# First query block prepared in two halves, c fetched first, one tile normalized by GpSimd: a change at the start of an attention kernel

## The chip, the core and the metric

The kernel runs on one core of a Trainium2 chip. The metric is the time of one execution in device microseconds. TensorE's granted clock, the share of full speed that the profile shows it to have been given, is listed for every run. Each ratio is between runs of the same rounds on the same chip; the profiled runs that are set side by side come from several jobs on different chips. A transfer has "landed" when all of it is there. PE is TensorE's matmuls, PEld its weight loads, DVE is VectorE, ACT is ScalarE, POOL is GpSimd, SP is the sync engine; "SPq" and "ACTq" are the queues from which those engines issue transfers.

## The reference

A block with adaptive layer norm: `c` (512 values) gives six vectors; attention over the last 512 keys of a cache (32 query heads, 8 key heads), then an MLP. Only the first steps matter here:

```python
mod = (silu(c) @ w_mod).reshape(1, 6, 1, -1)            # sa, ca, ga, sb, cb, gb
h = layernorm(x) * (1 + ca) + sa                         # x: 2048 x 512
x = x + ga * attention(h, k_cache, v_cache, wq, wo)      # q = h @ wq, 32 heads of 128
...                                                      # second layer norm, MLP with relu
```

## The kernel before

Queries are worked on in four blocks of 512. For each of 4 x 32 units (block, head) a step does score matmuls and exp, the projection of a later unit, and the products with v. Before the first step can start, the first block has to be normalized, transposed, modulated and projected. A helper records every operation and puts a wait on whatever wrote its inputs; each engine works in order (VectorE came to the three silu operations only at 7.62, behind the statistics, though the exponential they read had ended at 4.91). `warm(n)` puts n matmuls without use on TensorE, so that it is not idle.

```python
for i in range(2):                                       # x tiles 0,1 on SP; tiles 2,3 on ACT
    dma(x_sb[:, 2*i:2*i+2, :], ..., eng=ACT if i else SP)
dma(c_row, ...)                                          # SP
load_wm01(0)                                             # w_mod, contraction rows 0-255: SP
load_wm01(1, ACT)                                        # rows 256-511: ACT
load_wq(0, 2, ACT); load_wq(2, 2); load_k(0); load_v(0)  # the rest on SP
...
warm(7); silu_exp(5); warm(9)        # c transposed on TensorE, exp on ScalarE
...                                  # ScalarE: mean and variance of tile t3 (the fourth tile)
ln_stat(0); ln_stat(1); ...; ln_stat(2); ...             # VectorE
silu_mul(5)                          # VectorE: +1, reciprocal, product -> sc_bf
for tl in range(3): ln_norm(tl)      # VectorE; tile t3 is normalized by ScalarE
fs = mod_cols_mm(0, QBK)             # 32 one-column matmuls: sc_bf with both halves of w_mod
...                                  # they stand around the transposes of tile 0
for tl in range(1, TPB):
    ln_tposes(tl, [0, 2]); warm(tl)
ln_mod_ps([0, 2], hT[0], R_hT[0], 1) # four modulations, 128x512: two on VectorE, two on ScalarE
q_mms(0); q_mms(1, 5)                # projections of units 0 and 1, copies to qT by ScalarE
```

The "modulation columns" below are the 32 one-column matmuls of `mod_cols_mm`. Every one of the first outputs needs all 512 rows, so both halves of w_mod.

## Time and profile before

| | before |
|---|---|
| time, median of the first three runs | 564.28 us |
| span of the profiled run | 562.5 us |
| TensorE busy | 98% of the span |
| modulation columns start | 8.25 us |
| first score matmuls start | 13.47 us |
| span behind the first scores | 549.0 us |

The prediction shows the lines this rests on. A line of the chain reads: start, length, what the end was waiting for then. A line of the timeline reads: start, length, engine, source line, operation, output<-inputs, shape, count, and in brackets how long the engine idled and what ended that.

### The profile page before, as it was taken

Reading aid. Unit: us, or ns where it says so; the run is one execution under the profiler, and the core shown is the slowest. Engines: PE = TensorE matmul, PEld = TensorE weight load, DVE = VectorE, ACT = ScalarE, POOL = GpSimd, SP = SyncE. Lnnn points to the kernel's source line nnn. Section 1 sums busy time; section 2 is a strip of 40 time slices with the busy share of each in tenths; the row PEclk is TensorE's granted clock in tenths of the full one; section 3 lists DMA queues with packets and bytes.
Section 4 is the critical chain, followed back from the end, with each engine's and each line's share of the span. In section 5 each row is a group of like instructions: output and inputs, shape, how many; then the busy total and the mean of one; then the engine's idle time right before and its main releaser. Section 6 shows DMA issues by size and latency. Waiting matters only on the chain.

```text
span 562.5 us, 9700 instructions
## 1 busy us (share of the span) xinstructions
PE 553.7 (98%) x4097; PEld 316.9 (56%) x4172; DVE 242.2 (43%) x533; ACT 350.4 (62%) x453; POOL 38.7 (7%) x42
## 2 busy tenths in 40 slices
PE   8999999999999999999999999999999999999998
PEld 3565555555555555555555555555555654444444
DVE  4444465533334655333346553333354448321134
ACT  5986666666666666666666666666666644432500
POOL 1000000003300000033000000330000000000000
PEclk9999999999999999999999999999999999999999
DMA  9778776421331247332523522121123220210001
GB/s 268 204 165 167 143 160 132 113 38 38 39 76 37 39 93 133 57 94 46 144 56 57 102 50 39 39 40 40 39 39 72 44 31 0 41 36 24 22 28 48
DMA packets 113310, 42.70 MB, mean 76 GB/s; under 512 B 93928, under 2 KB 112104, under 8 KB 113256
## 3 DMA queue, kind: packets, MB, share of 16 engines
q1 hardware_dynamic: 112024, 40.82, 35.2%
q10 hardware_dynamic: 1232, 1.15, 0.6%
q8 instruction: 35, 0.57, 0.5%
q14 instruction: 19, 0.16, 0.1%
HBM read 18.35 MB, written 2.10 MB: 36 GB/s over the span
## 4 chain that ended last, share of the span: by engine, by line
PE 97%; issue 1%; DMA 1%; DVE 1%
PE psS L1363 28%; PE psO L1363 26%; PE psQ L1363 23%; PE psW L1363 20%; DMA x<-in_A_x_dram 1%; DVE st L1373 0%; PE psS L1366 0%; DVE mv L1374 0%; DVE rstd L1574 0%; DVE PT L1673 0%; DVE PT L1675 0%; DVE tmp L1427 0%; DVE sc_bf L1428 0%; DVE tmp L1426 0%
## 5 line engine op out<-in xcount | busy, mean ns | idle before, releaser
L1482 ACT ACTIVATE PT<-psS 128x1024 bf16<-128x1024 f32 x256 | 262.6, 1028 | 129.5 <-PE psS L1363 129.4
L1363 PE MATMUL psS<-qT,kT 128*128 128x512 bf16 x509 | 151.1, 379 | 0.2
L1363 PEld LDWEIGHTS psO<-v,PT 128*128 128x128 bf16 x2048 | 126.6, 98 | 30.2
L1363 PE MATMUL psO<-v,PT 128*128 128x129 bf16 x2048 | 137.0, 220 | 0.0
L1363 PE MATMUL psQ<-hT,wq 128*128 128x512 bf16 x507 | 130.3, 379 | 0.1
L1492 DVE RECIPROCAL rinv<-psO 128x4 f32<-128x4 f32 x128 | 23.4, 183 | 233.1 <-PE psO L1363 233.1
L1363 PE MATMUL psW<-wo,oT 128*128 128x512 bf16 x451 | 117.9, 379 | 3.2
L1493 DVE TENSOR_TENSOR o<-psO,rinv 128x512 bf16<-128x512 f32 x128 | 88.5, 692 | 4.4
L1363 PEld LDWEIGHTS psQ<-hT,wq 128*128 128x128 bf16 x508 | 49.6, 98 | 60.7 <-issue 0.5
L1363 PEld LDWEIGHTS psS<-qT,kT 128*128 128x128 bf16 x512 | 49.6, 98 | 59.3 <-ACT PT L1482 0.7
L1474 ACT ACTIVATE qT<-psQ 128x512 bf16<-128x512 f32 x127 | 75.2, 592 | 0.5 <-PE psQ L1363 0.5
L1662 ACT ACTIVATE wq<-psS 128x512 bf16<-128x512 f32 x56 | 33.4, 597 | 49.6 <-PE psS L1363 49.6
L1363 PEld LDWEIGHTS psW<-wo,oT 128*128 128x128 bf16 x512 | 45.0, 98 | 32.9 <-DVE acc L1515 1.2
L1515 DVE TENSOR_TENSOR acc<-psW,acc 128x512 f32<-128x512 f32 x48 | 33.2, 691 | 6.7 <-PE psW L1363 6.7
L1363 PE MATMUL psO<-wmw,wq 128*128 128x512 bf16 (+1 forms) x164 | 32.7, 352 | 0.3
L1518 POOL TENSOR_TENSOR acc<-acc,gaf 128x512 f32<-128x512 f32 x12 | 15.3, 1272 | 168.7 <-DVE acc L1515 168.7
L1379 POOL TENSOR_TENSOR rstd<-rstd,cst 128x4 f32<-128x4 f32 x7 | 7.1, 1012 | 265.3 <-DVE rstd L1378 265.3
L1363 PE MATMUL psS<-h2T,wmw 128*128 128x512 bf16 x110 | 25.2, 379 | 0.1
L1673 DVE TENSOR_TENSOR PT<-psO,gbf 128x512 f32<-128x512 f32 (+1 forms) x12 | 7.5, 624 | 40.4 <-PE psO L1363 40.4
L1363 PEld LDWEIGHTS psO<-wmw,wq 128*128 128x128 bf16 x168 | 15.4, 98 | 16.5
L1363 PE MATMUL psS<-hT,wmw 128*128 128x512 bf16 x110 | 24.4, 379 | 0.1
L1373 DVE BATCH_NORM_STATS2 st<-x 128x6 f32<-128x512 bf16 x31 | 21.0, 678 | 4.8 <-DMA x<-in_A_x_dram 4.8
(73 smaller groups left out, 170.4 us busy)
## 6 DMA issues: line engine op xcount, KB each, us to landing
wo<-in_A_wo_dram SPq DMA_DIRECT2D x4, 1024.0 KB, 5.7
wq<-in_A_wq_dram SPq DMA_DIRECT2D x7, 512.0 KB, 5.7
wmw<-in_B_w_dram SPq DMA_DIRECT2D x14, 256.0 KB, 3.3
wmw<-in_w_mod_dram SPq DMA_DIRECT2D x5, 512.0 KB, 4.7
oT<-o SPq DMA_TRANSPOSE x128, 2.4
out_dram<-PT SPq DMA_DIRECT2D x15, 128.0 KB, 1.8
x<-in_A_x_dram SPq DMA_DIRECT2D x3, 512.0 KB, 4.1
v<-in_A_v_cache_dram SPq DMA_DIRECT2D x8, 128.0 KB, 4.8
```

The source lines that it names most:

```text
L1363: kb.op(PE, lambda e: e.matmul(out_ap, lhsT, rhs, start=start, stop=stop), reads=reads, group_writes=[R_b[k] for k in bk], signal=signal)
L1373: kb.op(DVE, lambda e: e.bn_stats(st[:, t, :], x_sb[:, t, :]), reads=[R_x[t]], writes=[R_st[t]])
L1379: kb.op(POOL, lambda e: e.tensor_tensor(rstd[:, sl], rstd[:, sl], cst[:, 0:1].to_broadcast([P, hi - lo]), op=ALU.pow), reads=R_rstd[sl] + ...
L1474: kb.op(ACT, lambda e: e.activation(qT[u % NQT][:, :], bank[bk], ACTF.Copy), reads=[R_b[bk]], writes=[R_qT[u % NQT]])
L1482: kb.op(ACT, lambda e: e.activation(PT[u % NPT][:, pr * 2:pr * 2 + 2, :], s_ps[pr][:, :, :], ACTF.Exp, scale=scale), reads=[R_b[pr * 2], R ...
L1492: kb.op(DVE, lambda e: e.reciprocal(rinv[:, u, :], o_ps[:, :, P]), reads=[R_b[5], R_b[6]], writes=[R_rinv])
L1493: kb.op(DVE, lambda e: e.tensor_tensor(o_sb[u % NOS][:, :, :], o_ps[:, :, 0:P], rinv[:, u, :].unsqueeze(2).to_broadcast([P, TPB, P]), op=A ...
L1515: kb.op(DVE, lambda e: e.tensor_tensor(acc[:, tl, :], bank[WBK], acc[:, tl, :], op=ALU.add), reads=[R_b[WBK], R_acc[tl]], writes=[R_acc[tl]])
L1518: kb.op(eng, lambda e: e.tensor_tensor(acc[:, tl, :], acc[:, tl, :], gaf[:, :], op=ALU.mult), reads=[R_acc[tl], R_ga], writes=[R_acc[tl]])
L1662: kb.op(ACT, lambda e: e.activation(h1T[b % 2][:, fc, :], bank[bk], ACTF.Relu), reads=[R_b[bk]], writes=[R_h1[b % 2][fc]], pre=all_events( ...
L1673: kb.op(DVE, lambda e: e.tensor_tensor(yt[i][:, c0:c1], bank[bk][:, c0:c1], gbf[:, c0:c1], op=ALU.mult), reads=[R_b[bk], R_gb], writes=[R_ ...
```

## The change

Its intent: get silu off VectorE's path by fetching c first; let VectorE, ScalarE and TensorE overlap on the first block by treating 256 queries at a time; take one normalization off ScalarE.

```diff
+    dma(c_row[:, :], c[0].rearrange("(c p) -> c p", p=P), "c", writes=[R_c], eng=ACT)
     for i in range(2):
         dma(x_sb[:, 2 * i:2 * i + 2, :], ..., eng=ACT if i else SP)
-    dma(c_row[:, :], c[0].rearrange("(c p) -> c p", p=P), "c", writes=[R_c])
     load_wm01(0)
     load_wm01(1, ACT)
-    load_wq(0, 2, ACT)
+    load_wq(0, 2)
...
-    warm(7)
+    warm(6)
     silu_exp(5)
-    warm(9)
+    warm(8)
...
+    silu_mul(5)
     ln_stat(0)
...
-    silu_mul(5)
-    for tl in range(3):
-        ln_norm(tl)
-    kb.op(ACT, ...)                 # tile t3 on ScalarE
+    ln_norm(0)
+    ln_norm(1)
+    kb.op(POOL, lambda e: e.tensor_scalar(xn[:, t3, :], x_sb[:, t3, :], s3[:, 1:2], rstd[:, t3:t3 + 1], op0=ALU.add, op1=ALU.mult), ...)
-    (columns around the transposes of tile 0; tiles 1 to 3 with warm(tl); ln_mod_ps; q_mms(0); q_mms(1, 5))
+    for f in mod_cols_mm(0, QBK):
+        f()
+    mod_cols_evac(0, QBK)
+    ln_tposes(0, TB[0]); ln_tposes(1, TB[0]); warm(1)
+    mod_half(0, 0, DVE); mod_half(0, 2, ACT); mod_half(0, 1, DVE); mod_half(0, 3, ACT)
+    ln_norm(2)
+    q_half(0, 0, CC_ORDER[:3], QBK)
+    ln_tposes(3, TB[1]); ln_tposes(2, TB[1])
+    q_half(0, 0, CC_ORDER[3:], QBK)
+    mod_half(1, 0, DVE); mod_half(1, 2, ACT); mod_half(1, 1, DVE); mod_half(1, 3, DVE)
+    q_half(1, 0, CC_ORDER, 5)
+    for u, bk in ((0, QBK), (1, 5)):
+        q_half(u, 1, CC_ORDER, bk); q_evac(u, bk)
```

More of the change, by code (lines that the diff above doesn't have):

```diff
@@ L1311, in build_fast @@
     R_st, R_mv, R_rstd = RL("st", NT), RL("mv", NT), RL("rstd", NT)
+    R_h0 = RL("h0", DC)
     R_s3, R_eps = Res("s3"), Res("eps")
@@ L1397, in ln_tposes @@
         for cc in range(DC):
-            bk = bks[cc // 2]
+            bk = bks[cc]
             o = (cc % 2) * 512 + tl * P
             tpose(bank[bk].bitcast(BF)[:, o:o + P], xn[:, tl, cc * P:(cc + 1) * P], [R_xn[tl]], [bk], cc == DC - 1)
-    def ln_mod_ps(bks, dst, R_dst, which):
-        o, r = (0, R_moda) if which == 1 else (2 * DC, R_modb)
-        for k in range(2):
-            for half, eng in ((0, DVE), (1, ACT)):
-                cc = half * 2 + k
-                src = bank[bks[half]].bitcast(BF)[:, k * 512:(k + 1) * 512]
-                sc, sh = modc[:, o + DC + cc:o + DC + cc + 1], modc[:, o + cc:o + cc + 1]
-                if eng is DVE:
-                    kb.op(DVE, lambda e, src=src, sc=sc, sh=sh, cc=cc: e.tensor_scalar(dst[:, cc, :], src, sc, sh, op0=ALU.mult, op1=ALU.add),
-                          reads=[R_b[bks[half]], r], writes=[R_dst[cc]])
-                else:
-                    kb.op(ACT, lambda e, src=src, sc=sc, sh=sh, cc=cc: e.activation(dst[:, cc, :], src, ACTF.Identity, bias=sh, scale=sc),
-                          reads=[R_b[bks[half]], r], writes=[R_dst[cc]])
     CC_ORDER = (0, 2, 1, 3)
@@ L1469, in q_mms, with q_evac @@
         b, h = units[u]
-        order = CC_ORDER if u < QA else range(DC)
-        for i, cc in enumerate(order):
+        for i, cc in enumerate(range(DC)):
             mm(bank[bk], wq_sb[:, cc, h * Dh:(h + 1) * Dh], hT[b % 2][:, cc, :], i == 0, i == DC - 1,
-               [R_wq[h], R_hT[b % 2][cc]], [bk], i == DC - 1)
+               [R_wq[h], R_hT[b % 2][cc]] + ([R_h0[cc]] if b == 0 else []), [bk], i == DC - 1)
+        q_evac(u, bk)
+    def q_evac(u, bk=QBK):
         kb.op(ACT, lambda e: e.activation(qT[u % NQT][:, :], bank[bk], ACTF.Copy), reads=[R_b[bk]], writes=[R_qT[u % NQT]])
@@ L1586, in build_fast @@
     rstd_pow(2, 4)
-    silu_mul(5)
-    for tl in range(3):
-        ln_norm(tl)
-    kb.op(ACT, lambda e: e.activation(s3[:, 3:4], s3[:, 1:2], ACTF.Copy, scale=rstd[:, t3:t3 + 1]), reads=[R_s3, R_rstd[t3]], writes=[R_s3])
-    kb.op(ACT, lambda e: e.activation(xn[:, t3, :], x_sb[:, t3, :], ACTF.Identity, scale=rstd[:, t3:t3 + 1], bias=s3[:, 3:4]),
-          reads=[R_x[t3], R_rstd[t3], R_s3], writes=[R_xn[t3]])
-    fs = mod_cols_mm(0, QBK)
-    for f in fs[:len(fs) // 2]:
-        f()
-    ln_tposes(0, [0, 2])
@@ L1597, in build_fast @@
-    for f in fs[len(fs) // 2:]:
+    ln_norm(0)
+    ln_norm(1)
+    kb.op(POOL, lambda e: e.tensor_scalar(xn[:, t3, :], x_sb[:, t3, :], s3[:, 1:2], rstd[:, t3:t3 + 1], op0=ALU.add, op1=ALU.mult),
+          reads=[R_x[t3], R_rstd[t3], R_s3], writes=[R_xn[t3]])
+    for f in mod_cols_mm(0, QBK):
         f()
     mod_cols_evac(0, QBK)
-    for tl in range(1, TPB):
-        ln_tposes(tl, [0, 2])
-        warm(tl)
-    ln_mod_ps([0, 2], hT[0], R_hT[0], 1)
+    HB = QB // 2
+    R_half = [R_h0, R_hT[0]]
@@ new lines, in build_fast, with mod_half @@
+    TB = [[0, 0, 2, 2], [1, 1, 3, 6]]
+    def mod_half(hf, cc, eng):
+        bk = TB[hf][cc]
+        o = (cc % 2) * 512 + hf * HB
+        src, dst = bank[bk].bitcast(BF)[:, o:o + HB], hT[0][:, cc, hf * HB:(hf + 1) * HB]
+        sc, sh = modc[:, DC + cc:DC + cc + 1], modc[:, cc:cc + 1]
+        if eng is DVE:
+            kb.op(DVE, lambda e: e.tensor_scalar(dst, src, sc, sh, op0=ALU.mult, op1=ALU.add), reads=[R_b[bk], R_moda], writes=[R_half[hf][cc]])
+        else:
+            kb.op(ACT, lambda e: e.activation(dst, src, ACTF.Identity, bias=sh, scale=sc), reads=[R_b[bk], R_moda], writes=[R_half[hf][cc]])
@@ new lines, in q_half @@
+    def q_half(u, hf, order, bk):
+        for cc in order:
+            mm(bank[bk][:, hf * HB:(hf + 1) * HB], wq_sb[:, cc, u * Dh:(u + 1) * Dh], hT[0][:, cc, hf * HB:(hf + 1) * HB], cc == CC_ORDER[0], cc == CC_ORDER[-1],
+               [R_wq[u], R_half[hf][cc]], [bk], cc == CC_ORDER[-1])
+    ln_tposes(0, TB[0])
+    ln_tposes(1, TB[0])
+    warm(1)
+    mod_half(0, 0, DVE)
+    mod_half(0, 2, ACT)
+    mod_half(0, 1, DVE)
+    mod_half(0, 3, ACT)
+    ln_norm(2)
+    q_half(0, 0, CC_ORDER[:3], QBK)
@@ L1604, in build_fast @@
+    ln_tposes(3, TB[1])
+    ln_tposes(2, TB[1])
+    q_half(0, 0, CC_ORDER[3:], QBK)
+    mod_half(1, 0, DVE)
+    mod_half(1, 2, ACT)
+    mod_half(1, 1, DVE)
+    mod_half(1, 3, DVE)
+    q_half(1, 0, CC_ORDER, 5)
+    for u, bk in ((0, QBK), (1, 5)):
+        q_half(u, 1, CC_ORDER, bk)
+        q_evac(u, bk)
     load_wq(R, R)
@@ L1606, in build_fast @@
     load_v(1)
-    q_mms(0)
-    q_mms(1, 5)
     kb.op(DVE, lambda e: e.tensor_copy(sc_rep[:, :, :], sc_bf[:, :].unsqueeze(2).to_broadcast([P, DC, P])), reads=[R_sc], writes=[R_screp])
```

## The prediction

> **What bounds the kernel now.** I read the page first: busy shares, the chain of work that ended last, then the chain of the first 20 us in order of time, and last the timeline of those microseconds engine by engine.
>
> ```profile
> PE 553.7 (98%) x4097; PEld 316.9 (56%) x4172; DVE 242.2 (43%) x533; ACT 350.4 (62%) x453; POOL 38.7 (7%) x42
> PE 97%; issue 1%; DMA 1%; DVE 1%
> ```
>
> The chain is TensorE for 97% of 562.5 us. Nothing in the diff takes work from that part; it touches only what runs before TensorE is fed. So the question is when the attention loop starts, and whether a shift of that start arrives at the end. Two steady steps show what the loop is paced by: the reciprocals of units 0 and 1 start at 18.14 and 20.77, so a step is 2.63 us, and one step of TensorE (four score matmuls, four projections, 16 value products) is about the same by the chain (0.86 + 0.86 + 0.91). From the first score matmul on it is a full pipe. A shift of its start should come through one to one.
>
> The chain of the first 20 us, cut to its turning points (start, length, what):
>
> ```profile
> 0.79 3.99 DMA x<-in_A_x_dram
> 4.80 0.70 DVE st L1373
> ...
> 8.03 0.17 DVE sc_bf L1428
> 8.20 0.05 issue
> 8.25 0.55 PE psQ L1363 x16
> ...
> 12.30 0.39 PE psQ L1363
> 12.69 0.86 PE psO L1363 x4
> 13.56 0.51 PE psS L1363 x2
> ```
>
> It starts with x landing at 4.78, runs through VectorE to 8.20 (statistics of three tiles, and the three silu operations last), then through TensorE. The timeline says what VectorE and ScalarE did at the two ends of that stretch:
>
> ```profile
> 7.62 0.16 DVE L1426 TENSOR_SCALAR tmp<-tmp 128x4 f32<-128x4 f32 x1
> 7.79 0.77 POOL L1577 TENSOR_TENSOR rstd<-rstd,cst 128x2 f32<-128x2 f32 x1 [0.28 <-DVE tmp L1426]
> 8.11 1.05 DVE L1384 TENSOR_SCALAR xn<-x,mv,rstd 128x512 bf16<-128x512 bf16 x3
> 8.91 0.81 ACT L1591 ACTIVATE xn<-x,s,rstd 128x512 bf16<-128x512 bf16 x1
> 10.80 1.45 ACT L1413 ACTIVATE hT<-psS,modc 128x512 bf16<-128x512 bf16 x2 [1.08 <-PE psS L1366]
> 10.80 1.00 DVE L1410 TENSOR_SCALAR hT<-psS,modc 128x512 bf16<-128x512 bf16 x2 [0.98 <-PE psS L1366]
> 12.73 0.60 ACT L1474 ACTIVATE qT<-psQ 128x512 bf16<-128x512 f32 x1 [0.48 <-PE psQ L1363]
> 13.47 0.59 PE L1363 MATMUL psS<-qT,kT 128*128 128x512 bf16 x2
> ```
>
> VectorE idles 0.98 us before modulating because all four tiles must be transposed first; then two full-width modulations on ScalarE (1.45 us) hold back the last projection matmul to 12.30; copy to qT at 12.73; first scores at about 13.45. That last number is the one to move.
>
> [...]the output products take 0.69 us at 512 columns, 0.42 at 256, 0.28 at 128, a fixed part near 0.15 us. [...]The trace has the two-input case only: 1272 ns for 128x512 f32. [...]the first normalization begins at 8.11 under a GpSimd power (7.79 to 8.56), and all three took 405 to 407 ns. [...]tiles 2 and 3 of x, now second there, lose roughly one issue (0.4 us).
>
> **The change part by part.**
>
> (1) *c first, silu done before x.* c was issued at 1.24 and used at 4.53; it is now issued at 0.78 with nothing ahead of it in its ring. By the same delay it lands by about 4.0, and I take 3.6, since it no longer queues behind x. The six warming matmuls end at 1.04 + 6 x 0.43 = 3.6. In the old trace the silu needs 0.38 us from the transposition to the end of the exponential and 0.57 for three VectorE operations, so about 1.0 in all: sc_bf at 4.65, just ahead of x at 4.78. That takes 0.5 us (7.62 to 8.11) out of VectorE's path. Tiles 2 and 3 landing at 5.4 in place of 4.98 is hidden for VectorE, which reaches tile 2 at 6.7, and ScalarE's rstd of tile 3 moves from 7.12 to about 7.5, still ahead of the power at 7.79. First normalization: 8.11 becomes about 7.65.
>
> (2) *Modulation columns first on TensorE.* The two w_mod transfers landed at 1.65 + 6.3 = 7.95 and 1.22 + 4.9 = 6.1. The late one is now issued 0.4 earlier, the early one 0.4 later; estimate 7.0 for both. The 32 one-column matmuls run at about 0.025 us each (16 in 0.55 with 0.16 of latency), so they are done by 8.0, before tile 0 is normalized (8.05). No cost on the path.
>
> (3) *Half 0.* Two normalizations, 0.32 apart and 0.41 long, end at 8.4; modc takes two operations (9.46 to 9.82 before, so 0.36) to 8.78; transposes of tile 1 end at about 8.85. Width 256 in PSUM: a 512-wide modulation is 542 ns; the SBUF normalization of equal width is 407. [...]VectorE: 8.90 to 9.63. ScalarE: 773 less 256 x 0.85 = 555 ns each, to 9.9.
>
> (4) *Tile 2 after half 0, tile 3 on GpSimd.* VectorE normalizes tile 2 at 9.56 to 9.97. GpSimd starts at 8.6 after its power; [...]replacing ScalarE's 0.29 + 0.81 that ended at 9.72. Transposes of tiles 3 and 2 end at 9.97 + 0.05 + 0.4 = 10.45.
>
> (5) *Half 1.* VectorE does three modulations: 10.5 to 11.56 (0.33 + 0.33 + 0.41); ScalarE one, to 11.05. The last half-width projection matmul starts at 11.62 and takes 0.27; qT copy 11.92 to 12.52 as before (0.60); scores 0.11 later, at 12.63 against 13.45.
>
> (6) *Extra work.* Eight 512-wide projections become sixteen 256-wide ones: same columns, eight weight loads more (98 ns each, beside other work), all before the loop. Three warming matmuls in front of, and five among, the transposes go; those filled idle time.
>
> Sum: 0.5 from silu, about 0.3 net from halves and the ScalarE modulation that was last: 0.8 us. x tiles 0 and 1 may land a little earlier with the other half of x 0.4 us behind, worth 0.1 by my choice. 564.28 - 0.9 = 563.4.
>
> **The rivals.** (A) *A transfer takes silu's place.* If c lands only at 4.3, VectorE, in order, starts statistics at about 5.3 and the 0.5 is given back: gain 0.3, time 564.0. For: c took 3.3 us before. Against: it was behind 256 KB. (B) [...]If GpSimd takes 1.3 us, as for the two-input form, it ends at 9.9[...]. (C) *TensorE's clock.* Fewer warming matmuls and longer gaps between 7 and 11.5 us could leave the array at half rate for a while in the loop; in the old trace weight loads of the warming matmuls are 0.43 apart until 6.74 and then closer, so the rate rose there. One such stretch of 3 us at half rate would cost some 1.5 us: 565. TensorE stays fed until about 7 as planned, so I give this one in twelve. (D) *The shift is absorbed later*, if the loop's start is held by k or wq. Against: k of group 0 landed at 2.62 + 7.2 = 9.8 and the first wq at 1.71 + 7.4 = 9.1; the latter must now be there by 9.36, and it is issued on a ring with less ahead. (E) *Better than summed*: x lands 0.3 earlier and the widths overlap more: 562.8.
>
> **Range and chances.** The three runs before spread over 0.9 us, as large as the gain. Between (A) to (C) above and (E) below, 562.6 to 564.3. Two per cent is 11.3 us, and all work up to the first scores is 13.4 us; no rival comes near, so within 2% has 0.98.
>
> **What would show it.** Right: sc_bf before the first statistics; first normalization near 7.65; 256-wide modulations of about 0.41 (VectorE) and 0.56 us (ScalarE); GpSimd's normalization below 1 us, ending before VectorE starts on tile 2; first scores near 12.6; all later steps shifted by the same amount and the span 0.8 to 0.9 shorter. Wrong: statistics starting after x has landed because of c; a GpSimd span over 1.2 us with TensorE waiting for it; projection or score matmuls of the first steps at half rate; first scores early but the reciprocal of unit 1 still near 20.8.

The sum in it comes to 0.9 us (0.5 from silu, 0.3 from the halves, 0.1 for x): 564.28 to 563.4, with the first scores at 12.63. VectorE's time at 256 columns (0.41 us, or 0.33 where the next one overlaps it, in steps 3 and 5) is the author's estimate. The 0.4 us that tiles 2 and 3 of x were to lose is, as an estimate, the length of the issue of x on that queue in the trace (0.41). ScalarE's 0.85 ns a column in step 3 agrees with the trace, as an estimate: 1028 ns at 1024 columns less 592 at 512. The 3 us of rival C are an assumption.

## The result

The changed kernel took 566.04 us in the median of six runs (565.44 to 567.11), the kernel before 564.74 in six of the same rounds (563.87 to 565.00). The ratio is 1.0028, 95% interval 1.0015 to 1.0040. A ratio here is the mean time of one kernel's runs over that of the other's runs of the same rounds, so not quite the ratio of the medians quoted. It is within 2%, but it is slower, and above the predicted range.

All six runs of the changed kernel had a mean granted clock of 0.994 to 0.997; the profiled run of the kernel before had 1.000.

The chain of the first 18 us of the changed kernel, to be held against the one before:

```profile
1.78 7.76 DMA wmw<-in_w_mod_dram
9.55 0.05 issue
9.59 0.90 PE psQ L1364 x30
10.49 0.48 PE psS L1367 x8
...
11.01 0.42 DVE hT L1594
...
12.36 0.32 PE psS L1367 x3
...
14.28 0.62 PE psQ L1364 x4
...
15.67 0.59 PE psS L1364 x2
```

The path no longer starts with x and VectorE. It starts with the second half of w_mod (`wmw`), issued at 1.78 on ScalarE's queue and landed at 9.55. First scores come at 15.67, against 13.47: 2.20 us later. The profiled runs are 566.52 and 564.26, so 2.26 apart: the shift of the start is the whole difference.

The timeline of the changed kernel says what went as planned and what did not:

```profile
4.63 0.68 DVE L1374 BATCH_NORM_STATS2 st<-x 128x6 f32<-128x512 bf16 x1
6.73 0.63 ACT L1557 ACTIVATE xn<-x 128x512 bf16<-128x512 bf16 x1 [2.63 <-DMA x<-in_A_x_dram]
7.75 0.72 DVE L1385 TENSOR_SCALAR xn<-x,mv,rstd 128x512 bf16<-128x512 bf16 x2
9.59 0.90 PE L1364 MATMUL psQ<-sc_bf,wmw 128*128 128x1 bf16 x30 [2.03 <-DMA wmw<-in_w_mod_dram]
9.82 0.77 POOL L1579 TENSOR_SCALAR xn<-x,s,rstd 128x512 bf16<-128x512 bf16 x1
11.01 0.73 DVE L1594 TENSOR_SCALAR hT<-psS,modc 128x256 bf16<-128x256 bf16 x2
```

Silu is done before the statistics (VectorE starts on x at 4.63 and normalizes at 7.75). But tiles 2 and 3 of x land at 6.73 in place of about 5.0, and TensorE stands waiting for w_mod until 9.59.

The busy time by stretch, first of the kernel before, then of the changed one. The columns: stretch, its length, busy time and number of instructions of PE, PEld, DVE, ACT and POOL, the granted clock, the share of the DMA engines (it adds up the time of packets, and can pass 1), GB/s.

```profile
6.00:8.00 2.00, 1.77 (x7) 0.49 (x5) 1.82 (x8) 1.10 (x3) 0.92 (x2) 1.00 1.14 346
8.00:10.00 2.00, 1.70 (x45) 1.64 (x47) 1.45 (x6) 1.11 (x2) 0.55 (x1) 1.00 1.41 201
12.00:14.00 2.00, 2.00 (x10) 0.73 (x9) 0.14 (x1) 1.25 (x3) 0.00 (x0) 1.00 1.13 329
```

```profile
6.00:8.00 2.00, 0.19 (x2) 0.13 (x2) 1.66 (x7) 1.20 (x4) 0.71 (x1) 1.00 1.06 367
8.00:10.00 2.00, 0.41 (x16) 0.41 (x17) 0.48 (x2) 0.83 (x3) 0.89 (x2) 1.00 1.56 163
10.00:12.00 2.00, 1.62 (x32) 1.19 (x30) 1.32 (x5) 1.00 (x2) 0.58 (x1) 0.77 1.14 285
12.00:14.00 2.00, 2.00 (x15) 1.69 (x14) 0.80 (x4) 0.59 (x2) 0.00 (x0) 0.50 1.19 303
14.00:16.00 2.00, 1.66 (x12) 1.03 (x11) 0.64 (x2) 1.07 (x2) 0.00 (x0) 0.87 1.10 347
```

Between 6 and 10 us TensorE was busy for 0.60 of 4 us, against 3.47 before. After that its clock falls to half (0.50 granted), from about 11.1 to 14.5 us in finer stretches, while the last transposes and projections are on the path.

So there are two suspects, one behind the other: late transfers, and a clock that fell at about 11.1 us, behind the wait for them.

### The profile page after: what moved, and what is told of

Read it like the earlier page. It is cut to its first block, busy times and chain, and to the rows that moved or that the text cites. A ratio compares the mean times of both kernels' runs of the same rounds, so it can differ in the third digit from the quotient of the medians.

```text
span 564.7 us, 9779 instructions
## 1 busy us (share of the span) xinstructions
PE 556.5 (99%) x4173; PEld 317.8 (56%) x4173; DVE 243.0 (43%) x536; ACT 349.5 (62%) x452; POOL 39.3 (7%) x43
## 4 chain that ended last, share of the span: by engine, by line
PE 98%; DMA 1%; DVE 0%; ACTq 0%; issue 0%; ACT 0%
PE psS L1364 28%; PE psO L1364 26%; PE psQ L1364 23%; PE psW L1364 20%; DMA wmw<-in_w_mod_dram 1%; PE psS L1367 0%; ACTq L1298 0%; ACT qT L1463 0%; DVE hT L1594 0%; DVE PT L1690 0%; DVE PT L1692 0%; PE psO L1367 0%
## 5 line engine op out<-in xcount | busy, mean ns | idle before, releaser
L1471 ACT ACTIVATE PT<-psS 128x1024 bf16<-128x1024 f32 x256 | 262.7, 1028 | 129.7 <-PE psS L1364 129.7
L1364 PE MATMUL psQ<-hT,wq 128*128 128x512 bf16 (+1 forms) x512 | 131.4, 379 | 0.4 <-DVE hT L1594 0.4
L1364 PE MATMUL psW<-wo,oT 128*128 128x512 bf16 x512 | 130.6, 379 | 0.0
L1364 PEld LDWEIGHTS psO<-wmw,wq 128*128 128x128 bf16 x168 | 15.4, 98 | 16.5
```

Of the source, the lines that this page charges most:

```text
L1364: kb.op(PE, lambda e: e.matmul(out_ap, lhsT, rhs, start=start, stop=stop), reads=reads, group_writes=[R_b[k] for k in bk], signal=signal)
L1471: kb.op(ACT, lambda e: e.activation(PT[u % NPT][:, pr * 2:pr * 2 + 2, :], s_ps[pr][:, :, :], ACTF.Exp, scale=scale), reads=[R_b[pr * 2], R ...
```

## The experiments

The theory, T: the new order of transfers makes the second half of w_mod (and tiles 2 and 3 of x) late; the wait lets the clock fall; both together make the start late, and all later work is shifted. Its rival, R1: the halves and the GpSimd tile themselves cost the time.

In this table, "columns" is the start of the modulation columns that need the second half of w_mod, "scores" the start of the first score matmuls, both from the profiled run; "time" is that same run's; "median" is that of all the run's fast executions. The ratio is to the kernel before in the same rounds, with its 95% interval.

| run | columns | scores | scores - columns | time | time - scores | median | ratio (interval) |
|---|---|---|---|---|---|---|---|
| before | 8.25 | 13.47 | 5.22 | 564.26 | 550.79 | 564.74 | |
| changed | 9.59 | 15.67 | 6.08 | 566.52 | 550.85 | 566.04 | 1.0028 (1.0015-1.0040) |
| e1_halves_only | 8.06 | 13.25 | 5.19 | 563.83 | 550.58 | 564.29 | 1.0005 (0.9991-1.0019) |
| e2_loads_only | 9.17 | 16.62 | 7.45 | 567.17 | 550.55 | 566.34 | 1.0040 (1.0024-1.0055) |
| e3_fill_wait | 9.98 | 15.16 | 5.18 | 565.88 | 550.72 | 565.88 | 1.0024 (1.0010-1.0037) |
| e4_wm1_on_sp | 7.65 | 12.78 | 5.13 | 563.39 | 550.61 | 565.43 | 1.0020 (1.0006-1.0034) |
| e5_fill_light | 7.89 | 13.92 | 6.03 | 564.34 | 550.42 | 564.50 | 1.0004 (0.9991-1.0018) |
| e6_fill_heavy | 8.09 | 13.51 | 5.42 | 564.28 | 550.77 | 564.58 | 1.0001 (0.9988-1.0015) |
| e7_wq0_on_act | 9.09 | 15.34 | 6.25 | 565.88 | 550.54 | 566.37 | 1.0033 (1.0017-1.0048) |
| e8_c_after_x | 8.75 | 15.16 | 6.41 | 565.78 | 550.62 | 565.83 | 1.0025 (1.0010-1.0041) |
| e9_c_on_pool | 11.31 | 16.96 | 5.65 | 567.77 | 550.81 | 567.74 | 1.0051 (1.0036-1.0067) |
| e10_silu_on_pool | 7.70 | 12.87 | 5.17 | 563.43 | 550.56 | 563.82 | 0.9985 (0.9969-1.0001) |
| e11_no_halves | 8.63 | 15.32 | 6.69 | 566.13 | 550.81 | 563.87 | 0.9992 (0.9978-1.0006) |
| e12_again | 7.65 | 12.83 | 5.18 | 563.85 | 551.02 | 563.57 | 0.9987 (0.9974-1.0001) |

Time minus scores lies between 550.4 and 551.0 in fourteen profiled runs, while the scores themselves move by 4.2 us. So whatever happens before the first scores is passed on one to one, and the columns of the table split a run: when w_mod lets the columns start, and what follows until the scores. The record gives the outputs of all twelve experiments as correct.

### Which part of the change costs

`e1_halves_only`: the changed kernel with the old transfers, old place of silu and old warming.

```diff
-    dma(c_row, ..., eng=ACT)                  # first on ACT
     ...                                       # x halves
+    dma(c_row, ...)                           # second on SP, as before
-    load_wq(0, 2)
+    load_wq(0, 2, ACT)
-    warm(6); silu_exp(5); warm(8)
+    warm(7); silu_exp(5); warm(9)
-    silu_mul(5)                               # before ln_stat(0)
+    silu_mul(5)                               # after rstd_pow(2, 4)
```

> The changed kernel with the order of transfers, the place of silu and the warming matmuls of the kernel before; halves and GpSimd normalization stay. Theory T (the new order of transfers makes the second w_mod half and x tiles 2 and 3 late, and the wait for them lets TensorE's clock fall): both transfers land as before (about 6.1 and 5.0 us), the clock stays at 1.0, first scores at about 13.0 (13.47 before), time 0.3 to 0.5 us below the kernel before, some 564.3. Rival R1 (the halves and the GpSimd tile are what costs: more instructions, a longer in-order path on TensorE): first scores at 15 or later, time near 566.

`e2_loads_only`: the kernel before with the opposite of these edits (new transfers, silu early, six and eight warming matmuls; full width).

> The kernel before with only the order of transfers, the place of silu and the warming matmuls of the change; full-width modulation and projection. Theory T: the second w_mod half lands at about 9.5 us, tiles 2 and 3 of x at about 6.7, the clock falls to half for one stretch of about 3.4 us, first scores at 15 to 15.7, time near 566. Rival R1: silu off the path gives 0.5 us, first scores at about 13.0, time near 564.3.

Both came out on T's side, though not with T's numbers: e1 gained nothing of the 0.3 to 0.5 us expected, and in e2 the scores came at 16.62, 0.9 us later than expected, with TensorE at half rate from about 8.6 to 15.4 us (granted clock 0.65 from 8 to 10, 0.50 from 10 to 14, 0.65 from 14 to 16), twice as long as expected. (The 3.4 us expected are the length of the changed kernel's stretch, 11.1 to 14.5.) The halves alone are not slower (ratio 1.0005, one of five runs with a clock of 0.997); the new transfers, together with the early silu and two warming matmuls less, are (1.0040). R1 falls. The landing in e2 (chain of its first 18 us) and the cost of the fallen clock there:

```profile
1.78 7.35 DMA wmw<-in_w_mod_dram
...
13.14 1.28 PE psW L1363 x3
```

Three warming matmuls, 0.65 us in the chain of the kernel before, take 1.28. Before, they ended at 11.41, when the first modulated tile had just come (10.80 + 0.54 = 11.34); in e2 that tile is there at about 13.72 and they end at 14.42. The filler that was almost free has become path, at half rate.

The halves alone are worth less than they look in e1. Scores come 0.22 earlier than before, but the columns start 0.19 earlier, because x happened to land at 4.61 in place of 4.78. From columns to scores it is 5.19 against 5.22.

### The transfers and the clock apart

`e3_fill_wait`: the wait stays, but TensorE is kept at work in it.

```diff
     warm(8)
+    warm(16)
```

> The changed kernel with 16 more warming matmuls after the eight (0.216 us each at full clock, so to about 9.4 us), which keep TensorE at work while it waits for w_mod. Theory T: the late landing at about 9.5 stays, the clock stays at 1.0, and what was at half clock (transposes of tiles 2 and 3, the last projections) is 0.8 us shorter: first scores at about 14.8, time near 565.2. Rival R2 (the half clock costs nothing, as those matmuls wait for VectorE and ScalarE anyway): first scores at about 15.6, time near 566. If the clock rises late in a run, the fillers themselves end late and the run is longer.

The clock was at 1.0 in all five runs. Three transposes of the second half, 0.32 us in the chain of the changed kernel, are at full rate in e3's:

```profile
12.50 0.17 PE psS L1367 x3
```

Scores came at 15.16, not 14.8, since the fillers ended at about 10 and held the columns back themselves; w_mod had landed at 8.9 in this run. From columns to scores it took 5.18, against 6.08 in the changed kernel: the fallen clock cost 0.9 us there, and R2 falls. That is read from one profiled run of each. In the times the fillers' own delay took most of it back (565.88 where 565.2 was expected; ratios 1.0024 and 1.0028). The rest of the loss stays.

`e4_wm1_on_sp`: both halves of w_mod on the sync queue, ahead of wq.

```diff
-    load_wm01(1, ACT)
+    load_wm01(1)
```

> The changed kernel with the second w_mod half issued on the sync queue right behind the first, ahead of wq; c and x tiles 2 and 3 stay first on ScalarE's queue. Theory T: both w_mod halves are in by about 7.5, tiles 2 and 3 of x still land at about 6.7 since they are still issued behind c; TensorE idles less, the clock stays up; first scores at about 13.2, time some 0.2 us below the kernel before (564.5). Rival R3 (c at the head of ScalarE's queue is the whole cause: everything behind it is late whichever queue w_mod is on): first scores past 14.5, time near 565.5.

The profiled run is the best single one of the early set, and its chain shows what the change could do:

```profile
1.72 5.89 DMA wmw<-in_w_mod_dram
...
7.65 0.90 PE psQ L1364 x30
...
9.06 0.42 DVE hT L1594
...
12.04 0.61 ACT qT L1463
...
12.78 0.59 PE psS L1364 x2
```

w_mod complete at 7.6, first scores at 12.78, 563.39 us with the clock at 1.0. But the other four runs had 0.997 and took 564.60 to 565.71. Same program, same chip: 565.3 on average with the clock fallen, 563.4 without. Not all of these 1.9 us need be the clock's: the four have no trace, so when their transfers landed is not known. In three other cases with runs of both kinds in one job, those with the clock at 0.997 took 1.0 (e1), 1.2 (e5) and 1.6 us (the kernel before, in e10's job) longer than the rest. R3 falls, as far as w_mod is concerned: in the traces of e5 and e6 too, with c first, the columns start at 7.89 and 8.09. But 564.5 had been expected with the clock up: one run beat that, and the four whose clock fell missed it.

`e5_fill_light` and `e6_fill_heavy`: e4 with more warming.

```diff
-    silu_exp(5); warm(8)
+    silu_exp(5); warm(9)          # e6: warm(12)
     ln_tposes(1, TB[0])
-    warm(1)
+    warm(2)                       # e6: warm(3), and warm(2) after ln_tposes(2, TB[1])
...
+    warm(1)                       # after the last q_half
```

> The run with both w_mod halves on the sync queue, with nine warming matmuls in place of eight before the modulation columns, two in place of one after the transposes of tile 1, and one after the last projection. Theory C (what is left there is the clock: four of five of its runs were at 0.997, one stretch of half clock, and 565.3 on average, the one at 1.0 took 563.39): the clock stays at 1.0 in most runs and those take about 563.4, first scores near 12.8. Rival: the spread there has another cause (landing times): clock at 1.0, but times still about 565.3.

> As the light one, with twelve warming matmuls before the modulation columns, three after the transposes of tile 1, two after those of tile 2, one after the last projection. Theory C: clock at 1.0 in all runs; the extra matmuls delay the path by up to 0.8 us where the clock rises late (up to 1.3 us more of warming at half clock) and by about 0.2 where it rises early: first scores 12.9 to 13.5, time 563.5 to 564. Rival: time about 565.3 in spite of the clock.

The clock stayed at 1.0 in four of five and in five of five runs, and the times came down to those of the kernel before (1.0004 and 1.0001), but not below. In the profiled run of e5 the next late transfer shows, in the timeline:

```profile
7.05 0.63 ACT L1557 ACTIVATE xn<-x 128x512 bf16<-128x512 bf16 x1 [2.94 <-DMA x<-in_A_x_dram]
10.14 0.90 POOL L1579 TENSOR_SCALAR xn<-x,s,rstd 128x512 bf16<-128x512 bf16 x1
11.09 0.34 PE L1367 MATMUL psS<-ident,xn 128*128 128x128 bf16 x3 [0.72 <-POOL xn L1579]
```

Tiles 2 and 3 of x, issued behind c, landed at 7.05 (6.77 in e6, 5.99 in e4); ScalarE's statistics of the fourth tile, the power on GpSimd and GpSimd's normalization follow in a row, and TensorE waits 0.72 us for the tile. So the gain of e4 is spent on that wait in e5. Both were expected lower (about 563.4, and 563.5 to 564): a clock that holds is not enough, and e4's best run owed its gain to an earlier x as well as to the clock.

### Why the transfers are late

The trace counts packets by queue (q1 is the sync engine's, q10 ScalarE's): packets, MB, the time of the packets as a share. In the stretch from 2.5 to 3.5 us, first the kernel before, then the changed one, which has no line for q10:

```profile
q1 hardware_dynamic: 77, 0.15, 49.7%
q10 hardware_dynamic: 79, 0.16, 45.3%
```

```profile
q1 hardware_dynamic: 102, 0.18, 91.8%
```

Before, the two halves of x, both issued at 0.79, move side by side. In the changed kernel tiles 2 and 3 are issued at 1.39, behind c (whose issue alone took 0.56 us), 0.6 us later; none of their packets moves before 3.5 us (q10's 8 packets between 1.5 and 2.5, 0.00 MB together, are c's). By then the sync queue is a transfer ahead, and from 3.5 to 6.5 us too it moves more than ScalarE's (0.61 against 0.41 MB).

`e7_wq0_on_act`: the changed kernel with `load_wq(0, 2, ACT)`. `e8_c_after_x`: the changed kernel with c second on ScalarE's queue, behind tiles 2 and 3 of x.

> The changed kernel with the first wq block back on ScalarE's queue, behind the second w_mod half; c stays first there. If the wq block issued ahead of it on the sync queue is what holds that w_mod half back: it lands at about 7.5 to 8, first scores at about 13.5 and time near 564.5 to 565. If being third on a queue that starts late is enough: it lands at 9 or later and time stays near 566.

> The changed kernel with c issued second on ScalarE's queue, behind tiles 2 and 3 of x. If c at the head is what starves that queue: tiles 2 and 3 land at about 5.0 again, the second w_mod half at 6.5 to 7.5, c at about 4.3, silu on VectorE's path (statistics start at about 5.2), first scores at about 13.3, time near 564.3. If w_mod's place in the order of issue (behind the first half and wq) is enough: it lands at 8.5 or later, first scores past 14.5, time 565.5 or more.

In e7 the columns, which e4 starts at 7.65, still wait for w_mod until 9.09:

```profile
9.09 0.92 PE L1364 MATMUL psQ<-sc_bf,wmw 128*128 128x1 bf16 x30 [2.19 <-DMA wmw<-in_w_mod_dram]
```

But only one of the two wq blocks moved: the other was still issued on the sync queue at 1.72, just before that half of w_mod at 1.78. In e8 tiles 2 and 3 are back at 5.0, but the second half of w_mod comes at 8.75 all the same, and c is not used before 4.72, so statistics start at 5.64. So c at the head is not the whole cause, and neither is the wq block that moved; the other one was not tested. What the runs have in common: the half of w_mod issued last (1.65 to 1.85 us) took 5.9 to 6.3 us to land when it was on the sync queue (before, e1, e4 to e6, e10, e12) and 6.9 to 7.8 on ScalarE's queue (changed, e2, e3, e7, e8). The profiled run of e11 is an exception (6.8 on the sync queue, columns at 8.63). Whether it is the queue is open. In all five runs with 6.9 to 7.8 a wq block had been issued on the sync queue just before; in e9 below, where both halves were issued at 1.25 and wq after them, they took 5.8 (sync) and 6.4 us (ScalarE).

In e8 the clock had never risen during this stretch:

```profile
7.37 0.15 PEld L1364 LDWEIGHTS psW<-ones 128*128 128x128 bf16 x1 [0.28 <-issue]
7.80 0.15 PEld L1364 LDWEIGHTS psQ<-sc_bf,wmw 128*128 128x128 bf16 x1 [0.28 <-DVE rstd L1563]
9.57 1.01 PE L1367 MATMUL psS<-ident,xn 128*128 128x128 bf16 x8
```

Weight loads 0.43 us apart (0.22 in the fillers of e3 from 5.85 on) are the half rate at which every profiled run starts: six to eight matmuls kept TensorE busy for 2.74 to 2.96 us of the first 4. Eight transposes take 1.01 us in place of 0.61 in e4. Yet the run is listed with a clock of 0.999, and the stretch from 0 to 4 us with 1.00 in all fourteen profiled runs: the listed mean doesn't count this half rate at the start.

### A version that probably gains

`e9_c_on_pool`: c issued from GpSimd, x and w_mod at once on the other two queues; the extra warming of e6 from the transposes of tile 1 on.

```diff
-    dma(c_row, ..., eng=ACT)      # first of all
+    dma(c_row, ..., eng=POOL)     # after the identity is built
```

> The changed kernel with c issued from GpSimd, so that both halves of x are issued at once and both w_mod halves right behind them on the two queues, wq after those; three warming matmuls after the transposes of tile 1, two after those of tile 2 and one after the last projection. If the changed kernel loses because of the order of its transfers and the clock alone, and its arithmetic is right: tiles 2 and 3 land at about 5.0, w_mod complete at about 7.0, c by about 4; first scores at 12.4 to 12.8, time about 563.2. If the transfers before wq can't be in before 7.7 whatever the order (1.5 MB of x and w_mod shared with other traffic): first scores at about 13.3 and time about 564.0.

A clear miss, at 567.74: c, 1 KB, issued at 1.46, was there only at 7.8; the share of the DMA engines was 1.05 from 4 to 6 us and 1.13 from 6 to 8. TensorE, idle for 4.0 us, is still at half rate at 11.3 (weight loads 0.43 us apart), though four of the five runs are listed with a clock of 1.0.

```profile
7.81 0.10 PEld L1408 LDWEIGHTS psO<-ident,c_row 4*128 4x128 bf16 x1 [4.92 <-DMA c_row<-in_c_dram]
```

`e10_silu_on_pool`, and once more unchanged as `e12_again`: transfers as in the kernel before, except that wq follows on the sync queue; silu is computed by ScalarE and GpSimd, so that VectorE never does it, however late c is; extra warming.

```diff
-    dma(c_row, ..., eng=ACT)                  # first of all
     ...                                       # x halves
+    dma(c_row, ...)                           # second on SP, ahead of load_wm01(0)
     def silu_mul(bk):
-        (VectorE: tmp + 1, reciprocal, product with cT)
+        kb.op(ACT,  ... e.activation(c_sb[:, :], cT, ACTF.Copy) ...)
+        kb.op(POOL, ... e.tensor_scalar(tmp, tmp, 1.0, None, op0=ALU.add) ...)
+        kb.op(POOL, ... e.tensor_tensor(tmp, tmp, minus_one, op=ALU.pow) ...)
+        kb.op(POOL, ... e.tensor_tensor(sc_bf, c_sb, tmp, op=ALU.mult) ...)
-    warm(6); silu_exp(5); warm(8)
+    warm(7); silu_exp(5); silu_mul(5); warm(7)
-    warm(1)                                   # after ln_tposes(1)
+    warm(3)                                   # and warm(2) after ln_tposes(2), warm(1) after the last q_half
```

> As the one with c on GpSimd's queue, but c second on the sync queue as in the kernel before (used at about 4.7), and silu computed by GpSimd and ScalarE (copy, add, power, product, to about 6.4) in place of three VectorE operations; 14 warming matmuls. VectorE starts on x when it lands, at 4.6 to 4.8, and never does silu: first normalization at about 7.6. w_mod complete at 7.0 to 7.5: first scores at 12.4 to 12.8, time about 563.2. If w_mod is complete only at 8: first scores at about 13.2, time about 563.9.

> The faster run once more, unchanged (halves, c second on the sync queue, silu on GpSimd, extra warming matmuls), to see whether its lead holds: 563.5 to 564.2 with the clock at 1.0 in every run, 0.5 us or more below the mean of the kernel before. If the lead was chance: equal within 0.2 us.

The chain of the first 18 us of e12:

```profile
1.66 5.86 DMA wmw<-in_w_mod_dram
7.52 0.14 issue
7.65 0.94 PE psQ L1366 x32
...
12.70 0.12 issue
12.83 0.59 PE psS L1366 x2
```

All ten runs had a clock of 1.0 and took 563.23 to 564.27 (means 563.77 and 563.63; the kernel before 564.87 and 564.28 in the same rounds). Both intervals just include 1, so a lead of 0.13 to 0.15% is likely rather than proved; two jobs give about the same. Part of e10's lead is the clock: three of the nine runs of the kernel before had fallen to 0.997 in those rounds (565.65 to 566.31). Against the other six, 564.35 on average, it is 0.58 us, and e12's is 0.65. In the profiled runs that much comes from the columns at 7.65 to 7.70 in place of 8.25, and no more can come from there: they again start when w_mod lands. The expected 12.4 to 12.8 and 563.2 of e10 were not quite reached.

`e11_no_halves`: the kernel before with the transfers and the silu of e10 and 14 warming matmuls, no halves.

> The kernel before (full-width modulation and projection, tile 3 normalized by ScalarE) with the transfers and the GpSimd silu of the run that was faster, and 14 warming matmuls. If the halves are what turns an earlier silu into time: tile 3's normalization on ScalarE (ending near 9.7 as before) still gates all four transposes, first scores at about 13.4, time as the kernel before within 0.2 us. If silu off VectorE is worth its 0.5 us alone: first scores at about 12.9 and 0.5 us below the kernel before.

This one doesn't decide. Its profiled run is an outlier (566.13; scores at 15.32 after late columns and, by the length of its transposes, 0.59 to 0.63 us for four against 0.38 in the kernel before, at half rate); the other four took 563.36 to 564.35, on average 563.85, 0.2 us above e12's 563.63. A difference of 0.2 us is within the noise of five runs, so what the halves are worth beside this silu stays open.

## Why the prediction was wrong

By its own steps.

- **What bounds the kernel: right.** A shift of the first scores arrives at the end one to one (time minus scores, 550.4 to 551.0 in all runs). Its rival D, that a shift would be absorbed later, falls.
- **Step 1, c and silu: right in VectorE, wrong in a side remark.** c was used at 3.71 (3.6 assumed), the first normalization came at 7.75 (7.65 said), the statistics started before the old time. But "Tiles 2 and 3 landing at 5.4" was 6.73, and rstd of tile 3 came at 8.86 in place of 7.5 with it. The author's estimate that the tiles lose roughly one issue (0.4 us) is where this went wrong: 0.6 us of issue became 1.7 us of landing in this run (tiles 2 and 3 landed at 5.99 to 7.05 in e3 to e6). It was not yet on the path here: GpSimd had tile 3 done at 10.59, before VectorE normalized tile 2 at 11.65.
- **Step 2, w_mod: this is the step that failed.** "The late one is now issued 0.4 earlier, the early one 0.4 later; estimate 7.0 for both." The first was near (7.2, by the first two columns at 7.37); the second, issued 0.56 us later than before (1.22 to 1.78), landed at 9.55 in place of 6.1. Old landing times were shifted by about the shift of their issue, as if the transfers were independent. In the traces the queues take from each other: in the stretch from 2.5 to 3.5 us each moved about half before (77 and 79 packets), and the sync queue, which was issued first, all of it after (102 packets). "No cost on the path" became the path: the half-width modulations started at 11.01, 2.1 us after the 8.90 that was said.
- **Steps 3 to 5, the halves and GpSimd: the durations were right.** 0.41 us for VectorE at 256 (0.41 said), 0.56 for ScalarE (555 ns), 0.77 for GpSimd (below 1 us said). The working of VectorE's 0.41 and GpSimd's own figure had no source in a trace; for VectorE the two traces give it afterwards: 542 ns at 512 columns and 406 at 256 leave, as an estimate, 270 ns that don't depend on the width. From the first half-width modulation to the first scores the sum says 8.90 to 12.63, 3.73 us; e4 took 9.06 to 12.78, 3.72.
- **Step 6, the warming that went: wrong.** (Two, not "three", went in front of the transposes: 7 + 9 became 6 + 8.) "Those filled idle time" is true of the time they filled, but filled time also held the clock (1.0 in all five runs of e3). In the changed kernel it fell after the wait of step 2; that less warming is enough without that wait, e4 against e5 and e6 suggest (fallen in four of five runs, then in one and in none, in another job). In the changed kernel the same 3.73 us took 4.66 (11.01 to 15.67), 0.93 more. With the 2.1 of step 2 that is 3.04, the whole distance from 12.63 to 15.67.
- **The sum: mis-sized even with the transfers repaired.** The 0.5 of silu and 0.3 of the halves overlap with a limit that was in the old profile: w_mod landed at 7.95 then, 0.25 us before silu was done at 8.20. Removing silu uncovers it. What is left is 0.55 to 0.60 from earlier columns (8.25 to 7.65 or 7.70), and that only because w_mod itself landed earlier in e4, e10 and e12, and 0.03 to 0.09 from the halves (5.22 against 5.19 in e1 and 5.13 in e4). So e4's best run had 0.69 of the 0.84 us that the sum gave up to the scores. That its time, 563.39, meets the predicted 563.4 is in part luck: its end came 0.18 us sooner after the scores than in the kernel before.
- **The rivals.** A named a transfer in place of silu, but the wrong one (c, which was in time). C named the clock with one chance in twelve; it fell in all six runs of the changed kernel, and in e3 its absence was worth 0.9 us. It fell before the loop and not in it, and after a wait for w_mod that C did not have; and C's own 565 lay outside the range, which ended at 564.3. B did not happen in the changed kernel; in e5 the tile was waited for, but because x was late (7.05), not because GpSimd was slow (0.90 us). Where the two engines normalized at the same time, one took longer: in e6 VectorE's, begun inside GpSimd's (9.85 to 10.62), took 0.62 us in place of 0.41; in e5 VectorE began first (10.07), and GpSimd's took 0.90 in place of 0.77. Of E one half happened and did not help: tiles 0 and 1 of x landed at 4.0 in place of 4.78, but VectorE was still at silu until 4.6, and then w_mod set the path.

Open: why the w_mod half that is issued last takes about a microsecond longer when it is on ScalarE's queue (the queue itself, or the wq block issued just before it), and which stretch of idle TensorE makes the clock fall. e3 and e6 show only that filling the idle time kept it up (1.0 in five of five runs each). In e7 it fell at about 9.6 us (0.90 from 8 to 10, 0.50 from 10 to 12), after a single wait of 2.2 us (6.9 to 9.09) with TensorE busy before and after it; in the changed kernel the longest wait was 2.0 us, with TensorE busy for only 0.60 of 4 us. What share of work holds the clock was not shown.

## What to carry to other kernels

When an operation is taken off the path, look up the landing time of every transfer that the next operation needs; here one stood 0.25 us behind the one removed, and moving an issue by 0.6 us moved landings by 1.7 us (x) and 3.4 us (half of w_mod). At the start of this kernel the order of issue was the schedule, so check each transfer's landing after every reordering, not only the one that was moved. Idle TensorE had a price here that showed only later (0.9 us from the columns to the scores, changed kernel against e3): before taking warming matmuls out, see whether the granted clock holds in several runs, not in one.
